# A convolution and a routed mixture of experts on one core: 74 single expert slots beside the output chunks, in ten groups, three pieces at fixed places of each step

## Chip, core, metric

One NeuronCore of a Trainium2 chip. The metric is the device time of one execution in microseconds. The kernel before was timed three times: 1799.66, 1805.89 and 1805.27 us, median 1805.27 us. TensorE (PE) multiplies matrices, VectorE (DVE) and ScalarE (ACT) work elementwise, GpSimd (POOL) issues the indirect transfers here, and SyncE (SP) issues the plain ones. Each engine executes its own instructions in the order in which the program was written, and waits on semaphores for the others.

## What is computed

```python
# attention part: a long causal convolution per channel
u = x * v                                   # x, v: (4, 11456, 128)
h_filt = relu(pos_emb @ w1) @ w2 * exp(-0.01 * pos)[:, None]
y = irfft(rfft(u, n=2*S) * rfft(h_filt, n=2*S))[:S]
x = (x * y).reshape(4 * 11456, 128)
# mixture of experts, one expert of eight for each token that is computed
do_compute = x @ w_skip > 0
out = x.copy()
logits = x[do_compute] @ w_gate
e_idx = argmax(logits);  gate_w = softmax(logits)[e_idx]
for e in range(8):                          # w1: (8, 128, 1024), w2: (8, 1024, 128)
    h = relu(x[mask_e] @ w1[e])
    out[mask_e] = x[mask_e] + gate_w * (h @ w2[e])
```

About half of the 45824 tokens are computed by an expert, and which ones is known only while the kernel runs.

## The kernel before

The convolution is a block transform of three blocks of 3840 positions. `first_phase` and `freq_phase` transform forward, multiply and transform half of the way back; they are not touched by the change. `out_phase` then works through 32 chunks of 3 blocks, 96 steps in all. In each step `product` makes one block of the last transform on TensorE (L1066) and multiplies it with `x` on DVE into `xm` (L1067); `turn` transposes it (L1079, copied by ACT at L1081), `score` makes the gate and skip scores (L1087, copied by ACT as `lt` at L1089), `score2` transposes those (L1093, L1096), and `store` writes the rows to `out`. These follow each other one step apart. Once a chunk, `choose`, `gate`, `count`, `total`, `ranks`, `route`, `spread`, `collect` and `write` choose an expert for each token, count, rank and sort the tokens, and write a list of the chunk's rows by expert to `lists`.

Tokens reach the experts in **slots**: up to 256 tokens of one expert. After some chunks a table is made (`Experts.table`) of the full slots that have come together so far: `KNOWN` lists (chunk, how many units, slots in a unit). Then `reach` and `find` compute where a slot's rows stand, `name` has POOL look them up (L652, an indirect read of `lists` into `ids`), and `gather` has POOL fetch the rows (L686, two indirect reads of `out` into `xt` for a slot; there are 14 `xt` buffers, and up to 12 slots are fetched ahead). After the experts' matmuls, `gated` (L763, DVE) adds, and two indirect writes of POOL (L757) put the rows back.

**Early slots** are worked beside the chunks by the generator `early_slots`. A slot is four pieces between its `yield`s:

1. ACT copies the expert's second weight (`wd`, L808); the first half of the up-projection (L751 to L753, 12 matmuls of 256 columns in a split format, into the two `mh` banks of PSUM); two `relu` copies by ACT (`h`, L774).
2. The second half, two more `relu` copies; ACT's half of the next slot's weight split (`ws`, L723); the transposition of the next slot's rows (L740) into an `mh` bank and its copy (`hl`, L742).
3. DVE's half of that split (L746, L728); the first half of the down-projection in fp32 (L823).
4. The second half; `gated`, and the two stores.

If the next slot has not been gathered by then, it is prepared in six more pieces. **Late slots** come after the chunks (`late_slots`), with up- and down-projection in the split format (L751 to L753, L872 to L874) and larger buffers: 22 pairs (two slots of one expert, 512 columns) and 20 singles. In all there are 29 early slots, 44 slots in pairs and 20 singles: 93.

The order around the change is written out in `out_phase`: `steps` holds for each step the functions with their rank. `work`, the generator of early slots, is advanced by one piece at rank 0, behind `product`, and by one more at the end of a step whenever the credit of 0.4 a step has reached one: 1.4 pieces a step. `name` issues one lookup a step. When the steps are done, a loop finishes tables and names with one piece a turn, and then the remaining early pieces run alone.

Of the kernel before, what the change touches and what calls it, by code (L numbers as in the profile page):

```python
# [37 lines left out]
ZR = 128 - 2 * K1  # L38
C, X, LP = H2 + 1, slice(64, 64 + E), 64

KNOWN = ((3, 4, 1), (5, 5, 1), (8, 8, 1), (13, 12, 1), (23, 12, 2), (29, 10, 2))
NKNOWN = sum(n * u for c, n, u in KNOWN)
NEARLY = sum(n for c, n, u in KNOWN if u == 1)
LEAD = 6
# [1 line left out]
FEND = 2  # L46
KS = 4
QX = 4
PACE = 1.4
START = (0, 4, 7)  # L50
STORE = 7
C4 = 2
# [3 lines left out]
XT = 14  # L56
GATHERS = 12
FETCH = 4
NLATE = 64
NLAST = NEARLY + NLATE - NKNOWN  # L60
NTAB = 188


def units():

    at, found = 0, []
    for n, u in [(n, u) for _, n, u in KNOWN] + [(NLAST, 1)]:
        found += [list(range(k, k + u)) for k in range(at, at + n * u, u)]
# [410 lines left out]
class Experts:  # L479
# [164 lines left out]
    def sum(self, ps, pool, name="at"):  # L644
        at = pool.tile([128, 1], I32, name=name)
        with self.nc.allow_low_precision(reason="whole numbers that float32 holds"):
            self.nc.vector.tensor_reduce(at, ps, axis=AX.X, op=ALU.add)  # L647
        return at
# [346 lines left out]
def out_phase(tc, i, out, zd, ex, consts):  # L995
# [6 lines left out]
    with (  # L1002
# [3 lines left out]
      with (  # L1006
# [191 lines left out]
        cr, written, checks, base = {}, [], {}, 0  # L1198
        for c, n, u in KNOWN:
            checks[c - 1] = base, n, u  # L1200
            base += n * u
        work = ex.early_slots(eb, ob, eps, bank[2])
# [10 lines left out]
        def reach():  # L1213

            for _ in range(2):
                if not groups:
                    return
                ch, b, n = groups[0]
                if b not in ex.spots or ch not in written:
                    return  # L1220
                k = turn_of.get(b, 0)
                spot, parts = ex.spots[b]
                new.append((b + k, ch, ex.reached(spot[:, k:k + 1]), parts[:, k]))
                turn_of[b] = k + 1
                if k + 1 == n:
                    groups.pop(0)

        def find():
            for k, (s, ch, ge, step) in enumerate(new):
                ex.places(ge, step, where[k])  # L1230
                found.append((s, ch, where[k]))
            new.clear()

        def name(most=1):
            for s, ch, ps in found:
                queue.append((s, ex.sum(ps, keep, f"at{s}"), ch))
            found.clear()
            for _ in range(min(most, len(queue))):
                ex.issue(queue.pop(0))
# [3 lines left out]
        def tabled(half):  # L1243

            if tables and (half or started):
                started.append(1)
                if next(tables[0], tables) is tables:
                    tables.pop(0)
                    started.clear()
# [23 lines left out]
        steps = {}  # L1273
# [8 lines left out]
                steps.setdefault(first(ch) + lag, []).append((order, f, (ch,)))  # L1282
        for t in steps:
            steps[t] += [(-1.5, tabled, (0,)), (-1, name, ()), (4.6, find, ()), (4.7, tabled, (1,)), (7.5, reach, ())]
        credit = 0.0
        for t in sorted(steps):
            todo = sorted(steps[t], key=lambda v: v[0])
            if all(rank for rank, _, _ in todo):
                todo = sorted(todo + [(0, lambda: None, ())], key=lambda v: v[0])
            for rank, f, args in todo:  # L1290
                f(*args)
                if rank == 0:
                    next(work, None)
            credit += PACE - 1
            while credit >= 1:
                credit -= 1
                next(work, None)
        while tables or groups or new or found:
            tabled(0)
            name()  # L1300
            next(work, None)
            find()
            tabled(1)
            reach()
        for _ in work:
            pass
# [3 lines left out]
def program(tc, i, out):  # L1310
# [6 lines left out]
    with tc.tile_pool(name="mc", bufs=1) as mc:  # L1317
        wf = mc.tile([128, 2 * E * F], F32, name="wf")
        fi = First(nc, i, x1d, x1f, mc, wf)
        spare = wf[:, fi.used:]  # L1320
        c3 = mc.tile([128, 2, 128], F32, name="c3")
        first_phase(tc, fi)
        nc.scalar.dma_start(c3, i["c3"])
        later = {}

        def prepare():

            later["ex"] = Experts(tc, i, out, lists, mc, wf)
            yield
            later["consts"] = out_consts(nc, i, mc)  # L1330
            for e in range(E):
                if e % 2 == 0:
                    yield
                later["ex"].weights(e, 0)

            for e in range(E):
                if e != 1:
                    yield
                later["ex"].weights(e, 1)
        freq_phase(tc, nc, i, fi, zd, c3, spare, prepare())  # L1340
        out_phase(tc, i, out, zd, later["ex"], later["consts"])
# [54 lines left out]
```

## Time and profile before

The profiled execution took 1805.72 us; its span, from the first to the last instruction, is 1803.8 us.

| part of the span | us | what runs |
|---|---|---|
| 0 to 748 | 748 | transforms, before the output stage |
| 748 to 828 | 80 | first steps of the output stage, no slots yet |
| 828 to 1264 | 436 | steps with early slots beside them |
| 1264 to 1343 | 79 | end of the routing, tables, last early slots |
| 1343 to 1642 | 298 | 22 late pairs |
| 1642 to 1804 | 162 | 20 late singles and the end |

Over the whole span TensorE is busy for 88%, POOL 56%, DVE 66%, ACT 46%. An average over such different stages says little; the stages have to be read one by one, by how long a stretch takes and how much of it TensorE works. The profile's ends of matmuls are modelled, so a busy TensorE is not one at its peak, and the granted clock stands beside it.

### The profile page before, as it was taken

The page shows a single profiled execution, that of the slowest core. Times are in us where ns is not written, and L with a number is a line of the kernel's source. Part 1 is how long each engine was busy: PE and PEld are TensorE (multiplying, and loading weights), DVE is VectorE, ACT ScalarE, POOL GpSimd, SP SyncE. Part 2 cuts the span into 40 slices and gives each one's busy share as a digit, 9 for nine tenths or more (in the row PEclk, how much of TensorE's full clock was granted, in tenths as well). Part 3 has the DMA queues.
Part 4 walks back from the last instruction along what each step waited for, and adds up shares of the span by engine and source line. Part 5 has one row for each costly group of instructions (what it writes and reads, how often), then busy time and mean ns, then how long its engine had stood idle before and what let it go on. Part 6 is the DMA issues. An engine that isn't in the chain of part 4 may idle for free. (4 is left out here: it accounts for less than half of the span.)

```text
span 1803.8 us, 26628 instructions
## 1 busy us (share of the span) xinstructions
PE 1589.3 (88%) x8528; PEld 1009.3 (56%) x8528; DVE 1198.3 (66%) x2524; ACT 822.6 (46%) x1740; POOL 1012.6 (56%) x664
## 2 busy tenths in 40 slices
PE   6987999999999999687789778979768898899897
PEld 2543444444444444234566556756656776787896
DVE  1326778887887999477566545756656665577685
ACT  3553545455454444233344334535424554455664
POOL 1005888888887888203453432234565676677563
PEclk9987999999999999899899889989889998999899
DMA  7999999999997898798566645755211111111110
GB/s 257 321 347 337 375 381 363 347 321 331 346 323 256 227 340 222 213 334 249 162 214 183 211 141 188 229 172 179 72 22 26 34 40 36 34 40 36 28 35 19
DMA packets 188665, 360.34 MB, mean 200 GB/s; under 512 B 54794, under 2 KB 128988, under 8 KB 188516
## 3 DMA queue, kind: packets, MB, share of 16 engines
q1 hardware_dynamic: 169484, 318.63, 52.6%
q0 software_dynamic: 18144, 38.67, 7.5%
q10 hardware_dynamic: 896, 1.32, 0.3%
q8 instruction: 69, 1.13, 0.3%
q14 instruction: 72, 0.59, 0.1%
HBM read 215.50 MB, written 144.11 MB: 199 GB/s over the span
## 5 line engine op out<-in xcount | busy, mean ns | idle before, releaser
L757 POOL DMA_INDIRECT out<-o,ids x186 | 210.8, 1133 | 352.7 <-DVE o L763 292.6
L413 PE MATMUL ps<-y,c 128*128 128x512 f32 x720 | 331.7, 597 | 2.1 <-POOL y L473 1.4
L473 POOL TENSOR_TENSOR y<-y,p 128x2048 f32<-128x2048 f32 x60 | 272.2, 4537 | 70.8 <-DVE p L402 70.8
L686 POOL DMA_INDIRECT xt<-out,ids x186 | 191.8, 1031 | 77.3 <-issue 50.9
L861 DVE SCALAR_TENSOR_TENSOR hh<-hp,hh 128x1024 fp32r<-128x1024 f32 x128 | 155.9, 1218 | 116.8 <-ACT hh L860 94.9
L413 PEld LDWEIGHTS ps<-y,c 128*128 128x128 f32 x720 | 133.3, 190 | 175.3 <-issue 155.0
L402 DVE TENSOR_TENSOR p<-xp,g 128x1024 f32<-128x1024 f32 x240 | 217.4, 947 | 0.0
L402 DVE TENSOR_TENSOR y<-xp,g 128x1536 f32<-128x1536 f32 x120 | 210.7, 1756 | 4.1
L860 ACT ACTIVATE hh<-hp 128x1024 fp32r<-128x1024 f32 x128 | 131.9, 1031 | 135.9 <-PE hp L753 51.2
L414 ACT COPY z<-ps 128x512 f32<-128x512 f32 x180 | 105.5, 586 | 178.7 <-PE ps L413 167.4
L652 POOL DMA_INDIRECT ids<-lists,at x93 | 101.0, 1086 | 125.1 <-DVE at L647 97.7
L751 PE MATMUL hp<-hl,ws 128*128 128x512 f32 (+1 forms) x336 | 126.4, 376 | 28.3 <-DVE hh L861 13.3
L728 DVE TENSOR_TENSOR ws<-wf,ws 128x1024 fp32r<-128x1024 f32 x113 | 137.5, 1217 | 12.7 <-ACT ws L723 7.1
L474 POOL TENSOR_TENSOR y<-y,p 128x1024 f32<-128x1024 f32 x60 | 141.4, 2357 | 4.7
L823 PEld LDWEIGHTS bank<-wd,h 128*128 128x128 f32 x928 | 122.0, 212 | 36.5 <-issue 36.5
L823 PE MATMUL bank<-wd,h 128*128 128x128 f32 x928 | 133.3, 302 | 1.1 <-issue 1.1
L1066 PE MATMUL y<-zt,c 128*64 128x512 f32 x384 | 115.4, 665 | 15.7 <-issue 9.5
L1067 DVE TENSOR_TENSOR xm<-y,ox 128x512 f32<-128x512 f32 x96 | 66.5, 692 | 93.6 <-PE y L1066 47.5
L211 PE MATMUL ps<-wf,c 60*120 60x384 f32 x512 | 112.4, 534 | 11.6 <-DVE wf L194 11.2
L382 PE MATMUL xp<-x,wf 128*128 128x480 f32 x256 | 115.7, 576 | 7.1 <-issue 3.8
L723 ACT CAST ws<-wf 128x1024 fp32r x113 | 118.0, 1044 | 7.3 <-issue 1.8
L752 PE MATMUL hp<-hl,ws 128*128 128x512 f32 (+1 forms) x336 | 118.1, 351 | 1.0 <-issue 1.0
(188 smaller groups left out, 3102.9 us busy)
## 6 DMA issues: line engine op xcount, KB each, us to landing
wf<-xv SPq DMA_DIRECT2D x64, 768.0 KB
zt<-zd SPq DMA_DIRECT2D x64, 768.0 KB
x1d<-wf SPq DMA_DIRECT2D x64, 720.0 KB
x<-x1d SPq DMA_DIRECT2D x60, 768.0 KB
zd<-z SPq DMA_DIRECT2D x118, 384.0 KB
out<-xm SPq DMA_DIRECT2D x96, 258.0 KB
ox<-xo SPq DMA_DIRECT2D x96, 256.0 KB
x1f<-fx POOLq DMA_DIRECT2D x16, 720.0 KB
```

The lines of the kernel that those rows point to most:

```text
L402: nc.vector.tensor_tensor(o[:, :, :, j * KH:(j + 1) * KH].rearrange("p s a k b d -> p (s a) k b d"), x[:, None].broadcast_to([128, m, KH, ...
L413: nc.tensor.matmul(zps, c3[:, a, :], y[:, blk, a], start=(a == 0), stop=(a == 1))
L473: nc.gpsimd.tensor_tensor(y[:, 1:], y[:, 1:], p1, ALU.add)
L474: nc.gpsimd.tensor_tensor(y[:, 2:], y[:, 2:], p2, ALU.add)
L686: ins = nc.gpsimd.indirect_dma_start(out=xt[:, j], out_offset=None, in_=self.rows[0:have], in_offset=bass.IndirectOffsetOnAxis(ap=ids[:, j ...
L728: eng.tensor_tensor(w[:, 1], src[:, ds(self.where(eng, tb), F)], w[:, 0].bitcast(F32), ALU.subtract)
L751: nc.tensor.matmul(hp, w[:, 0, c], hl[:, 0], start=True, stop=False)
L752: nc.tensor.matmul(hp, w[:, 0, c], hl[:, 1], start=False, stop=False)
L757: ins = nc.gpsimd.indirect_dma_start(out=self.rows, out_offset=bass.IndirectOffsetOnAxis(ap=ids[:, j:j + 1], axis=0), in_=o, in_offset=Non ...
L823: nc.tensor.matmul(bank[:, j * D:(j + 1) * D], h[f // 2][:, f % 2, j * 128:(j + 1) * 128], wd[s][:, f * D:(f + 1) * D], start=(f == 0), st ...
L860: nc.scalar.activation(h[:, 0], hp, AF.Relu)
L861: nc.vector.scalar_tensor_tensor(h[:, 1], hp, 0.0, h[:, 0].bitcast(F32), ALU.max, ALU.subtract)
```

## The change

The table `KNOWN` gets ten groups of single slots, 74 in all, about eight after every third chunk; pairs are gone. 19 single slots are late (`NLATE`). The credit is replaced by `PIECES`: three pieces in each step, behind rank 0 (after `product`), behind rank 3.5 (after `score2`, `choose` and `spread`, before `turn`) and behind rank 7 (before `reach` and `store`). The loop after the steps advances two pieces a turn.

```diff
-KNOWN = ((3, 4, 1), (5, 5, 1), (8, 8, 1), (13, 12, 1), (23, 12, 2), (29, 10, 2))
+KNOWN = ((3, 4, 1), (5, 5, 1), (8, 8, 1), (11, 8, 1), (14, 8, 1), (17, 8, 1), (20, 8, 1), (23, 9, 1), (26, 8, 1), (29, 8, 1))
...
-PACE = 1.4
+PIECES = (0, 3.5, 7)
...
-NLATE = 64
+NLATE = 19
...
-        credit = 0.0
         for t in sorted(steps):
-            todo = sorted(steps[t], key=lambda v: v[0])
-            if all(rank for rank, _, _ in todo):
-                todo = sorted(todo + [(0, lambda: None, ())], key=lambda v: v[0])
-            for rank, f, args in todo:
+            for rank, f, args in sorted(steps[t] + [(r + 0.1, next, (work, None)) for r in PIECES], key=lambda v: v[0]):
                 f(*args)
-                if rank == 0:
-                    next(work, None)
-            credit += PACE - 1
-            while credit >= 1:
-                credit -= 1
-                next(work, None)
         while tables or groups or new or found:
             tabled(0)
             name()
             next(work, None)
             find()
             tabled(1)
+            next(work, None)
             reach()
```

TensorE in a step in the middle of the output stage (the 66th), before; rows are line, operation, output<-inputs and shape:

```order
L1066 MATMUL y<-zt,c_8614 64x512 x2
L823 MATMUL bank_4491<-wd,h 128x128 x8
L1093 MATMUL bank_4492<-ident,lt 128x128
L1079 MATMUL tp<-ident,xm 128x128 x4
L1140 LDWEIGHTS odd
L1140 MATMUL bank_4490<-ct,odd 96x1
L1087 MATMUL bank_4489<-xT,wg 32x128 x4
```

and the same step after the change, without its third piece:

```order
L1066 MATMUL y<-zt,c_9964 64x512 x2
L823 MATMUL bank_4491<-wd,h 128x128 x8
L1093 MATMUL bank_4492<-ident,lt 128x128
L823 MATMUL bank_4491<-wd,h 128x128 x8
L1079 MATMUL tp<-ident,xm 128x128 x4
L1140 LDWEIGHTS odd
L1140 MATMUL bank_4490<-ct,odd 96x1
L642 LDWEIGHTS reach_4479
L642 MATMUL bank_4490<-step_10499,reach_4479 128x2
L642 LDWEIGHTS reach_4480
L642 MATMUL bank_4490<-step_10499,reach_4480 128x2
L1087 MATMUL bank_4489<-xT,wg 32x128 x4
```

Where one piece (a half of the down-projection) stood behind the product, both halves stand in one step with only L1093 between them; behind the last row follow the twelve matmuls of the next slot's first piece. L642 is `find`, for two names.

ACT between the two halves of a slot's up-projection, in steps 60 to 65, before (`wd` is the weight copy, `h` the two relu copies of a half, `lg`, `xT`, `lt` and `ct` belong to the chunks):

```order
L808 COPY wd<-wf 128x1024
L774 ACTIVATE h<-mh 128x512 x2
L1119 ACTIVATE ee<-df 128x96
L1096 COPY lg<-bank_4492 128x36
L1081 COPY xT<-tp 128x512
L1089 COPY lt<-bank_4489 128x128
L1136 CAST ct<-bank_4489 96x1
L774 ACTIVATE h<-mh 128x512 x2
```

and a slot in the same place after the change:

```order
L808 COPY wd<-wf 128x1024
L774 ACTIVATE h<-mh 128x512 x2
L1151 COPY cr<-ct 96x128
L1096 COPY lg<-bank_4492 128x36
L774 ACTIVATE h<-mh 128x512 x2
```

A step's copies `xT` and `lt` no longer stand between the halves. In other slots all four copies of `h` follow one another directly, before the change and after it.

POOL's issues in the middle of the output stage, before (`out` are stores, `ids` name lookups, `xt` gathers):

```order
L757 DMA out<-o_4457,ids 49152x129 x2
L652 DMA ids<-lists,at_8131 128x2
L686 DMA xt_4446<-out,ids 128x129 x2
L686 DMA xt_4447<-out,ids 128x129 x2
L686 DMA xt_4448<-out,ids 128x129 x2
L652 DMA ids<-lists,at_8209 128x2
L652 DMA ids<-lists,at_8211 128x2
```

and after:

```order
L652 DMA ids<-lists,at_8410 128x2
L757 DMA out<-o_4455,ids 49152x129 x2
L686 DMA xt_4447<-out,ids 128x129 x2
L652 DMA ids<-lists,at_8412 128x2
L757 DMA out<-o_4456,ids 49152x129 x2
L686 DMA xt_4448<-out,ids 128x129 x2
L652 DMA ids<-lists,at_8554 128x2
L757 DMA out<-o_4457,ids 49152x129 x2
```

Six gathers in a row with three names around them became two gathers at a time, with a name and the two stores of a slot between.

## The prediction

> **What bounds the kernel now.** I read the page first: the engine totals, then the span in 40 slices of 45 us.
>
> ```profile
> PE 1589.3 (88%) x8528; PEld 1009.3 (56%) x8528; DVE 1198.3 (66%) x2524; ACT 822.6 (46%) x1740; POOL 1012.6 (56%) x664
> PE   6987999999999999687789778979768898899897
> PEclk9987999999999999899899889989889998999899
> ```
>
> TensorE is busy for 88% of the span. From slice 17, where the output stage begins, it is full in a few slices only, and the granted clock dips there too. The change touches nothing before that stage. So the question is what TensorE's idle time is worth in each stretch of the output stage, and the next view is the busy time by stretches, cut at the first product of a step or the first matmul of a unit. Columns: length, then PE, PEld, DVE, ACT and POOL busy (instructions), granted clock, DMA share, GB/s.
>
> ```profile
> 760.50:773.00 12.50, 12.01 (x98) 5.03 (x94) 6.91 (x20) 5.64 (x20) 0.00 (x0) 1.00 0.99 338
> 967.30:1016.20 48.90, 48.68 (x454) 36.24 (x450) 38.17 (x153) 25.25 (x61) 13.72 (x14) 1.00 0.70 217
> 1058.80:1126.40 67.60, 55.46 (x467) 40.71 (x466) 35.24 (x115) 28.24 (x66) 19.52 (x19) 0.95 0.52 165
> 1126.40:1191.00 64.60, 63.24 (x579) 46.72 (x575) 48.91 (x179) 33.19 (x85) 16.28 (x15) 1.00 0.70 222
> 1208.20:1263.60 55.40, 51.12 (x447) 37.52 (x446) 35.45 (x133) 25.63 (x64) 22.08 (x20) 0.97 0.50 156
> 828.10:1343.50 515.40, 419.04 (x3532) 314.62 (x3529) 312.46 (x1205) 214.39 (x504) 210.64 (x200) 0.91 0.54 167
> 1343.50:1641.60 298.10, 270.56 (x1195) 217.50 (x1196) 189.21 (x268) 148.64 (x172) 197.13 (x180) 0.95 0.13 34
> 1641.60:1781.00 139.40, 128.96 (x993) 123.40 (x992) 106.81 (x154) 86.95 (x115) 85.15 (x78) 0.96 0.12 31
> ```
>
> Two stretches, 967.3 and 1126.4, are TensorE from end to end at the full clock. In the others it stands still and its clock falls. The same stretches, counted by line, give what lies in each: L1066 is the product (four to a step; two more at the closing edge of a stretch belong to the next step), L751 the first term of a slot's up-projection (eight to a slot, or to a pair), L823 the fp32 down-projection of an early slot (32 to a slot).
>
> ```profile
> 760.50:773.00 12.50, 6.48 (x25) 1.20 (x25) 1.00 0.99 338
> 967.30:1016.20 48.90, 10.80 (x42) 1.99 (x42) 1.00 0.70 217
> 1058.80:1126.40 67.60, 12.26 (x44) 2.17 (x44) 0.95 0.52 165
> 1126.40:1191.00 64.60, 14.07 (x54) 2.62 (x54) 1.00 0.70 222
> 1208.20:1263.60 55.40, 11.69 (x42) 2.08 (x42) 0.97 0.50 156
> 828.10:1343.50 515.40, 81.43 (x284) 14.48 (x284) 0.91 0.54 167
> ```
>
> ```profile
> 967.30:1016.20 48.90, 8.72 (x28) 5.29 (x28) 1.00 0.70 217
> 1058.80:1126.40 67.60, 10.60 (x32) 6.57 (x32) 0.95 0.52 165
> 1126.40:1191.00 64.60, 9.85 (x32) 6.05 (x32) 1.00 0.70 222
> 1208.20:1263.60 55.40, 7.40 (x24) 4.54 (x24) 0.97 0.50 156
> 828.10:1343.50 515.40, 73.30 (x232) 44.96 (x233) 0.91 0.54 167
> ```
>
> ```profile
> 967.30:1016.20 48.90, 14.36 (x112) 13.03 (x112) 1.00 0.70 217
> 1058.80:1126.40 67.60, 15.66 (x113) 14.25 (x112) 0.95 0.52 165
> 1126.40:1191.00 64.60, 20.52 (x160) 18.61 (x160) 1.00 0.70 222
> 1208.20:1263.60 55.40, 17.18 (x128) 15.66 (x128) 0.97 0.50 156
> ```
>
> **The price of a step and of a slot.** Six early steps take 12.5 us, so 2.08 us each, without the per-chunk work (collecting, ranking, counting).
>
> ```profile
> 1062.34 0.49 PE L1187 MATMUL bank<-hl,hq 128*49 128x32 f16 x12
> ```
>
> Collecting is 0.49 us a chunk; with the shorter products I put 0.8 us a chunk, 0.27 us a step: a step costs TensorE 2.35 us. The stretch from 967.3 has ten steps and 3.5 slots (28/8 up, 112/32 down) and no idle time: (48.9 - 23.5)/3.5 = 7.26 us a slot.
>
> With these prices the stretch from 828.1 (71 steps, 29 early slots, some 10 us of chunk work behind the last product, an estimate) should take 167 + 211 + 10 = 388 us. It takes 515.4, so 128 us are lost, 4.4 us a slot. The pairs: 22 in 298.1 us, 6.8 us a slot. The singles: 19 in 139.4, 7.3 us each.
>
> **The change, part by part.** The 22 pairs and one of the 20 late singles disappear from the end: -298.1 - 7.3 = -305.4 us. Their 45 slots become early slots: +45 x 7.26 = +327 us. So in TensorE's work alone the change *adds* 21 us: a single early slot costs more than half a pair. What it can win is the 128 us now lost between 828.1 and 1343.5, if the added work fills that time and brings no such loss itself. Written from the start, 828.1 (start of the slots) + 167 (71 steps) + 74 x 7.26 = 537 + 10 + 154.9 (19 singles and the end: 1803.8 - 1641.6 - 7.3) = 1697 us + the new loss. The break-even loss is 107 us, 1.4 us for each of 74 slots. All else rests on that number.
>
> Fixed places: three pieces a step, four pieces a slot, so 0.75 slots a step. By the program order 51 slots have had their up-projection when the last product is issued (before: 24), 14 lie beside the rest of the chunk work and the naming, 9 run alone. POOL issues two gathers, one name lookup and two stores a slot as before, but most gathers of the 45 slots move from the late stage into this one, and with them the stores behind which SP's row transfers share the DMA engines (busy for 0.50 to 0.70 in these stretches, so I charge nothing for that). ACT, DVE and POOL I cost at nothing while TensorE covers them. ACT: 5.64/6 = 0.94 us a step, (25.25 - 9.4)/3.5 = 4.5 us a slot, so 4.3 us a dense step. DVE at worst, all above 6.91/6 counted as slots: (38.17 - 11.5)/3.5 = 7.6, so 6.9 us a step. POOL: 19.52/19 = 1.03 us an issue, five a slot, 3.9 us a step. All three lie under TensorE's 2.35 + 0.75 x 7.26 = 7.8 us. If that cover went, DVE is late next.
>
> The new loss. The stretches price the loss of the old order: 1126.4: 64.6 - 13 x 2.35 - 4.5 x 7.26 = 1.4 us, 0.3 a slot. 1208.2: 55.4 - 23.5 - 3.5 x 7.26 = 6.5, 1.9 a slot. 1058.8: 67.6 - 23.5 - 3.75 x 7.26 = 16.9, 4.5 a slot. What goes with it is the number of gathers:
>
> ```profile
> 967.30:1016.20 48.90, 2.37 (x2) 1.00 0.70 217
> 1058.80:1126.40 67.60, 8.17 (x8) 0.95 0.52 165
> 1126.40:1191.00 64.60, 4.10 (x4) 1.00 0.70 222
> 1208.20:1263.60 55.40, 6.11 (x6) 0.97 0.50 156
> ```
>
> 0.6, 0.9, 1.7 and 2.1 gathers a slot lose 0, 0.3, 1.9 and 4.5 us. In the changed kernel it is two. One such loss in order of time:
>
> ```profile
> 1100.89 0.38 PE L751 MATMUL mh<-hl,ws 128*128 128x256 f32 x1
> 1102.51 1.08 PE L1066 MATMUL y<-zt,c 128*64 128x512 f32 x4
> 1102.97 0.27 ACT L1089 COPY lt<-bank 128x128 f32<-128x128 f32 x1 [2.30 <-PE mh L753]
> 1103.79 1.04 ACT L808 COPY wd<-wf 128x1024 f32 x1 [0.56 <-issue]
> 1104.15 1.01 POOL L686 DMA_INDIRECT xt<-out,ids  x1 [0.31 <-issue]
> 1105.19 0.60 ACT L774 ACTIVATE h<-mh 128x512 f32<-128x512 f32 x1 [0.35 <-remote]
> 1105.84 0.58 PE L751 MATMUL mh<-hl,ws 128*128 128x256 f32 x1 [2.25 <-ACT wd L808]
> ```
>
> The first half of the up-projection (from 1100.89) fills both `mh` buffers. ACT empties them only behind `lt` and the weight copy `wd`, and TensorE, in order, waits 2.25 us. The two halves stood with only the product between them. By ACT's program order that held for 8 of 25 slots and holds for 17 of 53 now, a third as before; but of the others, which all had a whole step of chunk work there, 18 now have little more than the transposition L1093 between. Less covers ACT's lag. Queued behind the waiting L751 are the transpositions for `score` and `turn`, and DVE's `xm` and the routing wait for those.
>
> The long waits are a second sort:
>
> ```profile
> PE mh L740 <- ACT h L774: 34.3, 8, 10.8
> ```
>
> Eight waits, up to 10.8 us, in places where POOL issues four to six gathers in a row with names. Groups of eight make such rows shorter (two to four gathers), so I expect fewer. I bound the new loss by 0 and 4.5 us a slot and take 1.9, the stretch nearest in gathers and in the names beside them, for 65 slots, and 0.3 for the 9 alone: 123.5 + 2.7 = 126 us. Span 1697 + 126 = 1823; the execution lies 1.9 us above its span (1805.72 against 1803.8), and 0.5 us above the median 1805.27. Forecast 1825 us, 1.1% above.
>
> **The rivals.** *The queue stays full, faster.* More work between two waits could hide them, and the loss falls to the 0.3 us of 1126.4: 1697 + 22 + 2 = 1721 us; at half my rate, 1763. For it: two stretches show it, with the clock at 1.00. Against it: both have under one gather a slot, and no row shows two gathers a slot without loss.
>
> The clock belongs here: 0.91 over the stretch from 828.1, and 1.00 where TensorE never stands. [...]
>
> *It cancels.* At 1.45 to 1.73 us for each of the 65 slots the time lies within 0.5% of before (1796 to 1814), about what a measurement can tell from no change.
>
> *ACT's chain becomes the cycle, much slower.* Where every slot waits as in the stretch from 1058.8: 65 x 4.5 = 292, so about 1994 us; it decides from 3.3 us a slot, 1915. For it: that stretch has the gathers of the changed kernel. Against it: it holds one wait of the long sort.
>
> *It does not do what it says.* 23 of 74 slots are not beside products: already in the sum.
>
> **How the numbers follow.** Chances: 0.46 for the forecast (1814 to 1915), 0.28 for the faster rival, 0.16 for cancelling, 0.10 for above 1915. Faster 0.28, same 0.16, slower 0.56. The range leaves out the last tenth and the fast end below 0.75 us a slot (1750): 1750 to 1920 us.
>
> **What would show it.** In the changed profile: late singles from some 155 us before the end; steps of 7.8 us plus the loss; waits of L751 and L740 on ACT of about 2 us each in place of few long ones; granted clock above 0.95 between 828 and the last early slot. The forecast is wrong in its main step if steps take under 8.5 us (then the queue stays full), or if a wait on DVE or on a name takes the first place.

## The result, and the profile after

The changed kernel takes 1877.96 us (1875.39 to 1882.67 in four runs) against 1804.6 us of the kernel before beside it: a ratio of 1.044 (95% interval 1.0386 to 1.0493). The forecast was 1825 us, 1.1% slower. The profiled execution has a span of 1880.9 us. From its page, the engine totals, TensorE's busy tenths and its granted clock, in 40 slices of 47 us:

```profile
PE 1652.2 (88%) x9922; PEld 1098.2 (58%) x9922; DVE 1119.3 (60%) x2555; ACT 873.7 (46%) x1873; POOL 1013.8 (54%) x664
PE   5977999999999997868778979889888898989997
...
PEclk9988999999999999889889999899898999989998
```

TensorE is still not full in the output stage, though 45 more slots lie there. The busy time by stretches, cut at the first product of steps 23, 43 and 95 and at the end of the last early slot (columns as in the prediction):

```profile
826.70:1029.50 202.80, 152.44 (x1212) 117.57 (x1208) 94.51 (x336) 78.56 (x167) 68.47 (x65) 0.87 0.42 129
1029.50:1541.50 512.00, 441.90 (x3562) 352.30 (x3562) 258.22 (x928) 234.91 (x482) 232.41 (x219) 0.93 0.42 127
1541.50:1748.10 206.60, 185.42 (x1497) 170.45 (x1497) 85.88 (x290) 110.35 (x179) 124.61 (x117) 0.97 0.15 41
1748.10:1880.80 132.70, 118.29 (x985) 117.09 (x983) 103.95 (x143) 83.66 (x110) 78.46 (x64) 0.96 0.10 26
```

The down-projections (L823, 32 to a slot) in the first three of them:

```profile
826.70:1029.50 202.80, 54.91 (x384) 51.18 (x384) 0.87 0.42 129
1029.50:1541.50 512.00, 176.59 (x1249) 162.00 (x1248) 0.93 0.42 127
1541.50:1748.10 206.60, 91.47 (x737) 88.80 (x736) 0.97 0.15 41
```

So 12, 39 and 23 slots. With the prediction's prices (2.35 us a step, 7.26 a slot, 10 us of chunk work behind the last product) the loss is 202.8 - 20 x 2.35 - 12 x 7.26 = **69 us** in the first stretch, 512 - 52 x 2.35 - 39 x 7.26 = **107 us** in the second and 206.6 - 2.35 - 23 x 7.26 - 10 = **27 us** in the third: 203 us where the forecast had 126. The late part takes 132.7 us where the forecast had 154.9. TensorE's waits between 826.7 and 1541.5 (in all, times, longest):

```profile
PE mh L740 <- ACT h L774: 47.5, 29, 7.9
PE mh L740 <- DMA xt<-out,ids: 35.1, 8, 7.9
PE mh L740 <- issue: 14.9, 8, 3.0
PE mh L751 <- ACT h L774: 7.2, 12, 1.1
```

Two kinds stand in front: waits for ACT's `h`, as the prediction said, but nearly all at the transposition of the next slot (L740) and few between the halves (L751); and waits for gathered rows, which it did not name. One of the longest of the first kind, in order of time:

```profile
1434.84 0.42 PE L1087 MATMUL bank<-xT,wg 128*32 128x128 f32 x8
...
1435.17 1.00 POOL L652 DMA_INDIRECT ids<-lists,at  x1 [0.30 <-DVE tb L675]
...
1436.48 1.02 POOL L757 DMA_INDIRECT out<-o,ids  x1 [0.30 <-issue]
...
1436.62 0.28 PE L753 MATMUL mh<-hl,ws 128*128 128x256 f32 x1
1437.80 1.00 POOL L757 DMA_INDIRECT out<-o,ids  x1 [0.30 <-issue]
...
1439.11 1.04 POOL L686 DMA_INDIRECT xt<-out,ids  x1 [0.30 <-issue]
...
1440.46 1.02 POOL L686 DMA_INDIRECT xt<-out,ids  x1 [0.31 <-issue]
1441.78 1.00 POOL L652 DMA_INDIRECT ids<-lists,at  x1 [0.30 <-issue]
1442.58 0.27 ACT L1089 COPY lt<-bank 128x128 f32<-128x128 f32 x1 [6.98 <-remote]
1444.12 1.09 ACT L774 ACTIVATE h<-mh 128x512 f32<-128x512 f32 x2 [1.27 <-remote]
1444.77 0.29 PEld L740 LDWEIGHTS mh<-ident,xt 128*128 128x128 f32 x2 [8.07 <-ACT h L774]
```

TensorE's L1087 ends at 1435.26; ACT's `lt`, which needs nothing else, starts at 1442.58, and TensorE stands from 1436.9. ACT had nothing to do in between. The trace also records when each semaphore is raised: TensorE's, for L1087, at 1442.56. So TensorE's *signal* came 7.3 us after its work, while POOL issued one indirect transfer after another. (The ends of matmuls are modelled, but those behind L1087 start one after another until 1436.62, and its work on the array is taken to be done by then. The records do not tell a late write of its result from a late signal.) Matching the signals of TensorE with the ends of their instructions gives 76 of 919 matched ones that are over 1 us late, none of them while POOL issues nothing. That count is too low: it leaves out 55 raises that are on record. If each of these 974 is placed, in order and never before the end of its instruction, at least 171 are late. ACT's and DVE's signals beside POOL's issues are never over 0.1 us late.

### The profile page after: what moved, and what is told of

It is laid out like the page before. It is cut to its first block, busy times and chain, and to the rows that moved or that the text cites. A ratio compares the mean times of both kernels' runs of the same rounds, so it can differ in the third digit from the quotient of the medians.

```text
span 1880.9 us, 30007 instructions
## 1 busy us (share of the span) xinstructions
PE 1652.2 (88%) x9922; PEld 1098.2 (58%) x9922; DVE 1119.3 (60%) x2555; ACT 873.7 (46%) x1873; POOL 1013.8 (54%) x664
## 5 line engine op out<-in xcount | busy, mean ns | idle before, releaser
L757 POOL DMA_INDIRECT out<-o,ids x186 | 203.8, 1096 | 407.5 <-DVE o L763 237.1
L823 PEld LDWEIGHTS bank<-wd,h 128*128 128x128 f32 x2368 | 302.0, 207 | 48.5 <-issue 46.6
L823 PE MATMUL bank<-wd,h 128*128 128x128 f32 x2368 | 323.0, 294 | 6.0 <-issue 5.5
L686 POOL DMA_INDIRECT xt<-out,ids x186 | 197.1, 1060 | 88.9 <-issue 51.4
L774 ACT ACTIVATE h<-mh 128x512 f32<-128x512 f32 x296 | 171.7, 596 | 131.6 <-PE mh L753 78.3
L751 PE MATMUL mh<-hl,ws 128*128 128x256 f32 x592 | 185.0, 312 | 18.9 <-ACT h L774 11.5
L753 PE MATMUL mh<-hl,ws 128*128 128x256 f32 x592 | 169.4, 286 | 1.6 <-issue 1.1
L752 PE MATMUL mh<-hl,ws 128*128 128x256 f32 x592 | 168.2, 284 | 0.7 <-issue 0.5
L746 DVE TENSOR_TENSOR hl<-mh,hl 128x256 fp32r<-128x256 f32 x75 | 31.8, 424 | 215.6 <-ACT hl L742 142.8
L751 PEld LDWEIGHTS mh<-hl,ws 128*128 128x128 f32 x592 | 112.9, 191 | 65.4 <-issue 28.9
L1066 PE MATMUL y<-zt,c 128*64 128x512 f32 x384 | 120.4, 676 | 19.6 <-issue 9.6
L740 PE MATMUL mh<-ident,xt 128*128 128x128 f32 x150 | 37.1, 329 | 104.5 <-ACT h L774 52.7
```

What stands on the lines that cost most here:

```text
L686: ins = nc.gpsimd.indirect_dma_start(out=xt[:, j], out_offset=None, in_=self.rows[0:have], in_offset=bass.IndirectOffsetOnAxis(ap=ids[:, j ...
L751: nc.tensor.matmul(hp, w[:, 0, c], hl[:, 0], start=True, stop=False)
L752: nc.tensor.matmul(hp, w[:, 0, c], hl[:, 1], start=False, stop=False)
L753: nc.tensor.matmul(hp, w[:, 1, c], hl[:, 0], start=False, stop=True)
L757: ins = nc.gpsimd.indirect_dma_start(out=self.rows, out_offset=bass.IndirectOffsetOnAxis(ap=ids[:, j:j + 1], axis=0), in_=o, in_offset=Non ...
L774: nc.scalar.activation(h, hp, AF.Relu)
```

## The experiments

Losses are worked out as above. "Late" stands for TensorE's signals that are raised over 1 us after the end of their instruction, of those matched; "all placed" stands for the least number with every raise on record placed.

**Groups and places apart.** Two kernels make one half of the change each: the new `KNOWN` and `NLATE` with the old credit, and the new `PIECES` with the old groups.

The first (groups_only) is the kernel before with

```diff
-KNOWN = ((3, 4, 1), (5, 5, 1), (8, 8, 1), (13, 12, 1), (23, 12, 2), (29, 10, 2))
+KNOWN = ((3, 4, 1), (5, 5, 1), (8, 8, 1), (11, 8, 1), (14, 8, 1), (17, 8, 1), (20, 8, 1), (23, 9, 1), (26, 8, 1), (29, 8, 1))
-NLATE = 64
+NLATE = 19
```

and the second (pieces_only) the changed kernel with these four lines the other way round.

> New groups (74 early, 19 late), old pace of 1.4 pieces a step and one piece a turn behind the steps. Some 25 slots then lie beside the steps, 49 behind them. Theory A (a slot loses about 2.7 us wherever it is worked, as in the mean of the changed kernel): no change, 1870 to 1885. Theory B (the density of pieces makes the loss: slots used up as fast as they are named, and waits packed closer): steps as in the kernel before (828 to 1264), 49 slots alone at 7.5 us, 45 us of routing partly beside them, late part 133: 1795 to 1825.

> Old groups (29 early, 22 pairs, 20 late singles), three fixed places a step. Theory B (density): the loss beside the steps does not fall under the 128 us of before, since the slots of a group are worked off and the queue is empty between groups; 1800 to 1830. Theory A (2.7 us a slot): 29 x 2.7 = 78 us instead of 128, so 1755 to 1765. In both the pairs take 298 us as before.

Beside them on their chip, the kernel before took 1649.13 us (three runs) and not 1805. Groups alone took 1711.99 us, ratio 1.038 (1.0307 to 1.0451); places alone 1775.66, ratio 1.0765 (1.0688 to 1.0842). Neither trace has a single late signal, the largest lag being 0.1 us. So neither expectation in absolute numbers could hold; by the ratio both halves are slower. The groups' 1.038 is what theory A gave (1870 to 1885 of 1805), but by luck, since its loss of 2.7 us a slot is not there; the places' 1.0765 lies outside both theories. The first 361 us beside the steps with the old credit, and the first 20 steps with three places:

```profile
826.40:1187.20 360.80, 348.43 (x3204) 255.36 (x3200) 285.75 (x1130) 189.32 (x460) 189.88 (x178) 1.00 0.75 234
```

```profile
826.60:1022.30 195.70, 152.82 (x1199) 117.03 (x1195) 92.27 (x323) 78.83 (x167) 68.03 (x65) 0.84 0.44 133
```

Groups alone: 72 steps and 24.5 slots, 360.8 - 169.2 - 177.9 = 14 us of loss, clock 1.00; nearly all of the 63 us that this half costs is TensorE's own work on single slots in place of pairs (+59 by the prices below). Three places: 20 steps and 12 slots as in the changed kernel, 195.7 - 47 - 87.1 = 62 us, nearly the 69 of the first result, and without any late signal. TensorE stands still for 43 of them (195.7 - 152.8), and one line of its waits holds nearly all of that:

```profile
PE mh L740 <- DMA xt<-out,ids: 40.8, 14, 8.6
```

The other 19 us are the same work at the lower clock of 0.84: TensorE is busy for 152.8 us with what the prices put at 134.1.

**Both kernels once more, on other chips.** Unchanged copies, to see whether the late signals belong to the programs.

> The changed kernel, unchanged, beside the kernel before on one chip. The last four kernels ran beside a kernel before that took 1649 us, and no signal of TensorE in their traces was later than 0.1 us; in the first two traces signals came up to 12 us late while POOL issued indirect transfers. Theory C (the late signals belong to the chip, not to the kernel): where the kernel before takes about 1649, lags are at most 0.1 us, late singles and the tail take 133, and the time is 1697 - 22 + 60 to 80 of empty queue before step 44 = 1735 to 1760; where it takes about 1805, lags are back and the time is 1870 to 1885. Theory K (the lags come with these two programs): 1870 to 1885 anywhere.

> The kernel before, unchanged, for its trace. Theory C: at 1649 us its 22 pairs take 11.9 us each and its late singles 6.2, its loss between 828 and the last early slot falls from 128 us to 20 to 30, and its last product comes before 1195 (1264 in the first trace). Theory K: at 1649 us the lags are in the trace all the same, and the time is saved elsewhere.

> The changed kernel once more, for its trace, in case this is a chip on which the kernel before takes about 1650. There: no lag of TensorE's signals over 0.1 us, 1735 to 1760 (1697, 22 less for singles at 6.2, 60 to 70 of empty queue before step 44, 5 to 15 of the rest). On a chip where the kernel before takes 1800 to 1820: 1870 to 1905, with lags.

> The kernel before once more, for its trace. At about 1650: pairs of 11.9 us and singles of 6.2 throughout, last product before 1195. At 1800 to 1820: pairs of 13 to 14 on the mean, with lags.

| chip | kernel before, us | changed, us | ratio (95%) | late, before | late, changed |
|---|---|---|---|---|---|
| first result | 1804.6 | 1877.96 | 1.044 (1.0386 to 1.0493) | 136 of 811 | 76 of 919 |
| after_again | 1814.92 | 1904.44 | 1.0491 (1.0435 to 1.0547) | 122 of 819 | 113 of 910 |
| after_third | 1649.31 | 1754.2 | 1.0645 (1.062 to 1.0669) | 0 of 956 | 0 of 1028 |

The same programs take 7 to 9% less time where signals are not late. Theory C holds in that lateness does not come with the programs: on one chip, all traces of whole kernels have it or none has. But no chip is known to have been used at two times, so a state that comes and goes is not excluded; "a chip with late signals" below means the chip at that time. With all placed, 238 of 859 and 171 of 974 are late in the first result, 224 of 869 and 213 of 956 on the chip of after_again, none on the third. (The expectation for after_again put its time at 1870 to 1885 where the kernel before takes about 1805; with 1815 it was 1904.) On every chip the change is slower. The stretches of the changed kernel where no signal is late, cut at the same places:

```profile
821.20:1016.50 195.30, 150.76 (x1211) 116.23 (x1206) 94.44 (x337) 79.05 (x167) 68.61 (x65) 0.86 0.44 134
1016.50:1426.80 410.30, 407.29 (x3561) 330.44 (x3560) 259.53 (x928) 232.42 (x482) 234.42 (x219) 1.00 0.52 159
1426.80:1617.20 190.40, 179.37 (x1498) 165.43 (x1497) 85.87 (x290) 111.00 (x179) 127.08 (x117) 0.98 0.16 45
1617.20:1749.80 132.60, 118.24 (x984) 117.03 (x982) 103.85 (x143) 82.79 (x110) 78.42 (x64) 0.97 0.10 26
```

The losses are 61, 5 and 11 us (69, 107 and 27 in the first result). In the second stretch 52 steps and 39 slots take what their prices say, at a clock of 1.00. Its waits, from 826 to 1600:

```profile
PE mh L740 <- DMA xt<-out,ids: 40.7, 14, 8.7
...
PE mh L751 <- ACT h L774: 3.7, 12, 0.7
...
PE mh L740 <- ACT h L774: 0.3, 1, 0.3
```

The waits for ACT are gone with the late signals, from 47.5 to 0.3 us at L740, though the program's order is the same. The kernel before on that chip, its early slots from step 23 on and its 22 pairs:

```profile
824.80:1238.80 414.00, 396.77 (x3571) 297.29 (x3568) 312.43 (x1190) 215.91 (x512) 207.71 (x193) 0.98 0.68 212
1244.90:1506.70 261.80, 260.30 (x1216) 213.79 (x1217) 190.97 (x272) 151.44 (x177) 195.99 (x187) 0.99 0.16 40
```

Its early loss is 414 - 73 x 2.35 - 29 x 7.26 - 10 = 22 us in place of the 128 the prediction started from, and a pair takes 11.9 us in place of 13.6. Its last product starts at 1182.9 us, as expected before 1195. (The traced run of before_again took 1825.22 us, that of before_third 1649.46.)

**The first 20 steps.** Why rows are late there shows in POOL's queue, in the changed kernel without late signals:

```profile
874.43 0.99 POOL L757 DMA_INDIRECT out<-o,ids  x1 [8.48 <-DVE o L763]
875.72 0.98 POOL L757 DMA_INDIRECT out<-o,ids  x1 [0.30 <-DVE rs L1163]
...
877.01 1.04 POOL L652 DMA_INDIRECT ids<-lists,at  x1 [0.30 <-DVE tb L675]
...
879.79 1.01 POOL L686 DMA_INDIRECT xt<-out,ids  x1 [1.74 <-DMA ids<-lists,at]
881.11 1.00 POOL L686 DMA_INDIRECT xt<-out,ids  x1 [0.30 <-issue]
...
882.52 0.45 PE L740 MATMUL mh<-ident,xt 128*128 128x128 f32 x1 [4.40 <-DMA xt<-out,ids]
```

The lookup and the gathers of the next slot stand behind the two stores of this slot, which wait for its down-projection (POOL is idle for 8.48 us, until `o` is there). Nothing is fetched ahead, and TensorE waits 4.4 us for rows that it needs at once. Is it that slots are used up as fast as they are named? A kernel with 1.4 pieces a step before step 44 and three from there on lets names pile up first:

```diff
+        credit = 0.0
...
+            spots = PIECES
+            if t < 44:
+                credit += 0.4
+                spots = (0, 7) if credit >= 1 else (0,)
+                credit -= len(spots) - 1
...
```

> The changed kernel, but with 1.4 pieces a step before step 44 and three from there on, so that named slots pile up first. Theory B (three pieces use slots up as fast as they are named; TensorE waits for rows at the start of each group): the loss before step 44 falls from 60 to 70 us to under 20, and the time is 40 to 60 us under the changed kernel's on the same chip. If the loss belongs to three pieces a step as such, or moves to the later steps: within 15 us of the changed kernel.

> 1.4 pieces a step before step 44, three from there on. On a chip without late signals (kernel before about 1649, changed kernel 1754): theory B (empty queue) has the loss before step 44 fall from 61 us to 10 to 15, so 1705 to 1715. If three pieces at first were not the cause: 1740 to 1760. On a chip with late signals: about 1865 to 1880 again.

Both runs met chips with late signals: 1876.81 us where the changed kernel took 1904.44 (ratios to the kernel before 1.0332 and 1.0491), and 1858.83 on another (1.018, 1.0089 to 1.0271), just under the 1865 to 1880 expected. The first 20 steps on the second:

```profile
825.80:938.90 113.10, 96.14 (x846) 67.88 (x842) 79.43 (x310) 50.30 (x124) 55.49 (x50) 0.94 0.70 219
```

113.1 - 47 - 5.75 x 7.26 = 24 us of loss (6 slots by the up-projections in it, 5.5 by the down-projections), with late signals in it, instead of 69; on the first of the two chips it is 30 against the changed kernel's 69. It did not fall under 20 as expected there, and the gain in time was 28 us, less than the 40 to 60 expected. But 1.4 pieces a step lose 13 us in these steps even where no signal is late (the kernel before, 101.8 - 47 - 5.75 x 7.26), so most of what three places add there is gone.

**Which of POOL's transfers.** Parts of the changed kernel's indirect transfers are replaced by plain ones of SP, of the same size, from or to a fixed place. The slots' own rows are then not read, or their results not put into the output.

In `gather` (plain_gathers), in `store` (plain_stores), or in both (plain_both):

```diff
-            ins = nc.gpsimd.indirect_dma_start(
-                out=xt[:, j], out_offset=None, in_=self.rows[0:have],
...
+            nc.sync.dma_start(xt[:, j], self.i["xo"][0, 0, :, 0:W])
...
-        ins = nc.gpsimd.indirect_dma_start(
-            out=self.rows, out_offset=bass.IndirectOffsetOnAxis(ap=ids[:, j:j + 1], axis=0),
...
+        nc.sync.dma_start(self.aside[self.put % 256], o)
```

> The changed kernel, with each slot's two indirect gathers replaced by plain transfers of SP of the same size from a fixed place (the slots' own rows are not read; names and stores stay indirect). Theory S (TensorE's signals reach nobody while POOL issues indirect transfers, above all reads): lags of TensorE's signals over 1 us fall from 76 of 603 to under half as many, the loss between 1029 and the last product falls from 88 us to under 45, and the time to 1780 to 1820. Theory of the prediction (ACT's copies between the two halves of an up-projection): the loss there stays at 75 to 90 us, time above 1840. A theory of empty queues alone: only the 69 us before 1029 fall.

> The changed kernel with plain transfers of SP in place of the indirect gathers (the slots' own rows are not read). Where the kernel before takes about 1650: 1703 again. Where it takes 1800 to 1820: theory S (POOL's indirect reads hold TensorE's signals up) has lags over 1 us fall to under a third of the 113 of 910 in the changed kernel there, and the time to 1710 to 1760; if names and stores, or something else on that chip, hold them up as much: above 1800.

> Plain transfers of SP in place of the two indirect gathers of a slot (the slots' own rows are not read). Without late signals: 1701 to 1703 as twice before. With them (kernel before 1800 to 1820): if they go with indirect reads, 1720 to 1770 and few lags over 1 us; if with any of POOL's transfers, 1780 to 1840 and lags beside stores and names as frequent as in the changed kernel.

> Plain transfers of SP to a place aside instead of the two indirect stores of a slot (the rows' results are not put into the output; gathers and names stay). Without late signals: within 15 us of the changed kernel's 1754. With them: 1860 to 1890 if gathers and names make them, under 1830 if stores do as much.

> Gathers and stores both plain transfers of SP (rows neither read nor put into the output), only the 93 name lookups stay with POOL. Without late signals: 1690 to 1710. With them: 1700 to 1730 if lags need runs of POOL transfers, since names come singly; above 1760 if single names hold signals up as well.

(The 88 us in the first of these is mis-added; by the rows above it is 107. Its 76 late signals are counted there of 603, above of 919.) Twice plain gathers met a chip without late signals, 1702.64 and 1701.19 us, which says nothing of the lateness. It does say what the first 20 steps wait for. On the chip of after_third, one run of plain gathers took 1701.19 us where the changed kernel took 1754.2; its first 20 steps, and its wait for rows in them:

```profile
827.70:974.20 146.50, 138.94 (x1213) 108.81 (x1206) 93.65 (x337) 77.94 (x167) 39.61 (x37) 0.98 0.56 179
```

```profile
PE mh L736 <- DMA xt<-xo: 2.4, 3, 1.1
```

They lose 146.5 - 47 - 12 x 7.26 = 12 us instead of 61 (16 in the other trace), with the fetches at the same places of the program. (L736 is L740 there.) So rows are late by their way through POOL, where the indirect reads wait for the lookup (1.74 us in the queue above) and behind the stores, and not because the program asks for them too late. How much each part of that way takes is not shown.

The third run of plain gathers met late signals (kernel before 1824.48 us), and plain_stores and plain_both ran once each on the same chip. The 52 steps and 39 slots of the second stretch there, one row from each of plain_gathers_3, plain_stores and plain_both:

```profile
976.50:1432.90 456.40, 418.31 (x3561) 338.40 (x3560) 257.95 (x928) 232.15 (x482) 133.32 (x125) 0.98 0.46 143
```

```profile
1006.10:1439.00 432.90, 414.31 (x3561) 334.75 (x3560) 257.45 (x928) 231.70 (x482) 147.08 (x139) 0.99 0.53 151
```

```profile
982.40:1391.70 409.30, 407.12 (x3563) 330.35 (x3562) 256.77 (x928) 232.77 (x482) 49.34 (x49) 1.00 0.55 160
```

| kernel, chip with late signals | us | loss of the second stretch | late | all placed |
|---|---|---|---|---|
| changed (first result, another chip) | 1877.96 | 107 | 76 of 919 | 171 of 974 |
| plain gathers | 1759.79 | 51 | 35 of 911 | 85 of 942 |
| plain stores | 1785.05 | 28 | 52 of 910 | 73 of 925 |
| both plain, names alone left | 1702.11 | 4 | 0 of 961 | 0 of 965 |

The three below are single runs, and the changed kernel did not run on their chip; on that of after_again its second stretch lost 122 us. Either half takes away more than half of the loss, and names alone make no late signal, in the time that plain gathers take where none is late (1701.19). So it is not indirect reads as such. What fits them is how many transfers POOL issues without a gap; that there are fewer of them in all (three fifths with either half) would fit too. From the six traces of whole kernels with late signals, by the place of the transfer that POOL issues at the signal's time, counted from the start of an unbroken row (gaps under 0.6 us):

```
place in the row     none     1     2     3     4     5     6     7     8    9+
signals              1928   800   695   587   409   227   163    90    59   320
over 1 us late         14     7    36    95   100    94   100    49    38   136
share                  1%    1%    5%   16%   24%   41%   61%   54%   64%   43%
```

With all placed, and the place taken at the end of TensorE's instruction, the share rises in the same way: 5, 24, 43, 41, 61 and 73% from the first place to the sixth. At the same places it is 5, 21 and 37% (first to third) with plain gathers, whose rows hardly pass the fourth place, and 2, 8, 34, 42 and 79% with plain stores. So the place tells more than the number of transfers; with names alone, though, none of 48 signals at the second place is late, and the table is no experiment on the rows themselves. On chips without late signals rows are as long, and no signal is late.

**Breaking the rows.** POOL gets small memsets behind each indirect transfer beside the chunks: four of 261 numbers in the kernel before, one in the changed kernel.

```diff
+    def pause(self):
+        if self.pausing:
+            for _ in range(4):
+                self.nc.gpsimd.memset(self.rest, 0)
...
```

> The kernel before, with four small POOL memsets (about 1.2 us together, by 0.2 us for 128 numbers in the profile) behind each indirect transfer beside the chunks, so that no two follow one another; none in the late part. On a chip with late signals (kernel before 1805 to 1825): if unbroken rows make them, lags over 1 us between 828 and the last early slot fall to under a fifth of before (about 80), the last product comes before 1200 instead of 1264 to 1272, and the time falls by 60 to 100 us to 1715 to 1755. If the number of transfers makes them: 1800 or more. On a chip without: within 12 us of the kernel before, by what the pauses delay gathers.

> The changed kernel with one POOL memset of about 0.3 us behind each indirect transfer beside the chunks; none in the late part. On a chip with late signals (kernel before 1805 to 1825, changed kernel 1878 to 1904): if unbroken rows make them and a gap of some 0.8 us breaks a row, lags over 1 us fall from 76 to under 25 and the time to 1780 to 1830; if the number of transfers makes them, or the gap is too short: 1865 to 1915. On a chip without: 1745 to 1775, where POOL is no bound at 3.75 x 1.9 = 7.1 us a step of 7.8.

Both met chips without late signals, so the question they were made for stays open. They showed a price: the kernel before took 1851.03 us in place of 1648.23 (1.1229, 1.1196 to 1.1262), against "within 12 us".

```profile
L666 POOL MEMSET tab<- 1x261 int32 x828 | 256.1, 309 | 35.4
```

```profile
DVE o L772 <- DMA out<-o,ids: 166.8, 32, 19.9
```

With 1.4 us of memsets an issue took 2.9 us instead of 1.3; POOL fell behind, DVE waited 166.8 us for `o` buffers still being stored, and TensorE 62.8 us for DVE's `hh` (L759). With one memset the changed kernel took 1765.4 us, within the 1745 to 1775 expected, and 11 more than its 1754.2 on another such chip.

**Fewer early slots.** Late singles take 6.2 us each wherever signals are not late, pairs 5.95 a slot, early slots 7.26. So two kernels work fewer slots early: the changed one with 9 early slots and 84 late singles, and the kernel before with 17 early slots, 28 pairs and 0.9 pieces a step.

```diff
-NEARLY = sum(n for c, n, u in KNOWN if u == 1)
+NEARLY = 9
...
-KNOWN = ((3, 4, 1), (5, 5, 1), (8, 8, 1), (13, 12, 1), (23, 12, 2), (29, 10, 2))
+KNOWN = ((3, 4, 1), (5, 5, 1), (8, 8, 1), (13, 6, 2), (23, 12, 2), (29, 10, 2))
-PACE = 1.4
+PACE = 0.9
...
```

> The changed kernel with only its first 9 named slots worked early; the other 84 are late singles, 65 of them named and listed beside the chunks as in the changed kernel. Theory L (a late single takes 6.2 us, as in the changed kernel, an early one 7.3 and about 2.7 of loss): 828 + 71 steps x 3.2 + 9 x 7.3 + 45 of routing + 84 x 6.2 + 23 = 1710, with 1690 to 1740. Rival (late singles take 7.3 us as in the kernel before, 6.2 was the luck of 19): 1780 to 1800. Theory that slots hide beside the steps at all: slower than 1805.

> The kernel before with 17 early slots instead of 29, six more late pairs, and 0.9 pieces a step. Where a pair takes 11.9 us and an early slot 7.26, and TensorE stays the bound beside the steps (71 steps x 2.35 + 15 x 7.26 = 276, against 71 bare steps of 3.5 = 248): -12 x 7.26 + 6 x 11.9 = -16 us against the kernel before, 5 to 20 us faster. If early slots hide beside the steps: 30 to 70 us slower.

> 17 early slots, 28 pairs, 20 singles, 0.9 pieces a step, once more. Where pairs take 11.9 us (kernel before about 1650): 5 to 20 us faster than the kernel before, by -12 x 7.26 + 6 x 11.9. Where they take 13 to 14: 0 to 1.5% slower, as on the last chip (1.011).

Nine early slots: 1766.02 us beside 1649.13 (1.0706, 1.063 to 1.0782). Late singles took 6.2 us as in theory L, but its sum missed on the steps, by some 40 us in the first 16, where the nine slots lie, and 20 in the 56 without a slot. These took

```profile
982.00:1179.90 197.90, 154.86 (x1415) 77.10 (x1411) 178.28 (x776) 65.18 (x225) 60.92 (x60) 0.92 0.89 289
```

197.9/56 = 3.53 us each, with DVE busy for 90% and the DMA engines for 89%. TensorE needs 2.35 of them, so early slots at a slow pace are partly hidden: with groups alone, (360.8 - 72 x 3.53)/24.5 = 4.4 us a slot, less than any late slot. Seventeen early slots: 1643.69 us beside 1649.31 without late signals (0.9961, 0.9947 to 0.9975), 1835.07 beside 1814.92 with them (1.0109, 1.0071 to 1.0147). The first is 5.6 us faster, at the edge of the 5 to 20 expected; the second was neither 5 to 20 faster nor 30 to 70 slower. It is the one version that beats both kernels on some chip, by 0.4%; none was found that does on both sorts.

## Why the prediction was right in sign and wrong in size

- **Right: TensorE's own work.** 2.35 us a step and 7.26 a slot held to about 1% where nothing disturbs: 410.3 us against 405.3 for 52 steps and 39 slots. The count of 51 slots before the last product was right.
- **Wrong, the step that failed: "I bound the new loss by 0 and 4.5 us a slot and take 1.9", for 65 slots.** The measured loss beside the steps is 176 us for 51 slots, 3.4 a slot, and 27 behind them. More important, it is no rate that goes with gathers a slot. The four stretches that gave it go with late signals as well as with gathers: with all placed, 8 of 75 and 7 of 93 are late where 0 and 0.3 us a slot were lost, 9 of 66 where it was 1.9, 24 of 84 where it was 4.5. Two causes made the new loss.
  - *An empty queue*, in the first 20 steps, which lose 61 to 69 us on every chip with three places, 24 to 30 with two paces (signals late), and 12 to 16 with three places and plain gathers. Waits for rows are 41 of the 61, a lower clock (0.86) most of the rest. No rival named it; whether a slot's rows can come through POOL's queue in time when three pieces a step use them up was not asked.
  - *Late signals of TensorE*, by the difference of two chips 107 - 5 = 102 us in the second stretch and 16 behind it. TensorE stood still for 67 of the 102 more (70.1 against 3.0); in the other 35 the same matmuls took longer at the lower clock (441.9 us at 0.93 against 407.3 at 1.00). The prediction saw this ("places where POOL issues four to six gathers in a row with names") and expected fewer of them from shorter rows of gathers. But stores and names between did not break POOL's rows: in the wait shown above, two names, two stores and two gathers follow one another with 0.3 us between.
- **Refuted: ACT's copies as the cause.** The prediction read the wait at L751 as ACT's chain behind two halves with little between. Without late signals the changed kernel waits 3.7 us there in all. The wait that it shows in order of time began with a late signal too: L1087, whose scores `lt` copies, ends at 1100.96 us, its signal comes at 1102.95, and ACT's `lt` starts at 1102.97. The largest loss of the four stretches (24 of 84 signals late), the waits of up to 10.8 us (without late signals TensorE's longest in the kernel before is 3.0 us, from 826 to 1600), and part of the pairs' and singles' price (13.55 against 11.9 us, 7.3 against 6.2) go with the same disturbance. One sign of the prediction was seen all the same: 29 waits for ACT of 1.6 us on the mean at L740. A wait that is put down to ACT can be a late signal to ACT, so the sign did not tell the two apart. The other, steps under 8.5 us, was not seen there (9.8 to 10.1 us) but was where no signal is late (7.9 us in the second stretch).
- **Wrong: the late part**, -22 us. The 7.3 us of a late single came from a row with late signals; it is 6.2. The pair's 13.55 is 11.9.
- **The sum, mended.** Where signals are late: +21 us of slots' work, +75 of loss (203 against 128), -22 in the late part, and 3 left over: 77 in the spans. Where they are not: 45 slots x 7.26 against 22 x 11.9 + 6.2 is +59, loss 77 against 22 is +55, and -12 is left over: 102 in the spans. The gain that was possible, the 128 us of loss before, was 22 where no signal is late, and filling did not win it where they are.
- **The clock.** It was 0.87 in the first stretch and 0.93 in the second, not above 0.95, and the sum had no term for it. TensorE's waits, of about 2 us each in the forecast, were of up to 7.9 us; in the one shown above, the granted clock was 0.50 from 1439.8 to 1450.0 us. Where TensorE hardly stood (3.0 us from 1016.5 to 1426.8, without late signals) it was 1.00.
- **Rivals.** "The queue stays full" holds for 39 slots of the second stretch on a chip without late signals (0.1 us a slot), and even there the change is slower by 6.5%: its price stands in the slots' work and in the first 20 steps.

Open: what makes TensorE's signals late on some chips, and whether a gap in POOL's rows would prevent it. No run of a whole kernel had both added gaps and such a chip; names alone made none late there. Nor is the place in the row the whole of it: from the ninth place on, 3 of 63 signals were late in the first trace of the changed kernel and 16 of 32 in its second.

## What to carry to other kernels

Before a loss is read as the kernel's own, see whose signal the waiting engine waits for and when it was raised, and look at the same kernel on a second chip: by the difference of two chips, 156 of this one's 1805 us do not come with its program. When slots are to be used faster, ask first how many are ready at that moment, and whether the fetch of the next one stands in a queue behind a store that waits for this one. Price a slot against what it hides: beside steps that take 3.5 us without a slot, with DVE busy for 90% and the DMA engines for 89%, it cost 4.4 us at 1.4 pieces a step, alone 7.3, and as a late slot 6.0 to 6.2.

## What was not expected of the hardware

On the chips of three of the seven comparisons TensorE's semaphores were raised up to 13 us after the work, 655 of the 669 late ones while POOL issued indirect transfers, and on none of the others. In what was compared nothing else tells these chips apart: an issue takes 1.03 to 1.13 us on both, and the packets of the DMA queues 0.09 and 0.12 us on the mean. One thing goes with it: on these chips the trace holds 956 to 974 raises of TensorE's semaphore for the changed kernel's 1030 or so, and on the others all of them; the same for names alone, where none was late. ACT and DVE miss more there (in the first result's trace 1343 of ACT's 1570 and 1921 of DVE's 2203 raises of their main semaphores are left), and none of theirs is late. So missing records alone do not make an engine late. Whether the taking of the trace has a part in the lateness no run here shows, since every time was taken with a profile.
